# A one-token decode block: out projection in rows, PV of four groups in one PSUM tile, a fused mask-and-max, and a bf16 maximum broadcast

## The chip, the cores and the metric

The kernel runs on one core of a Trainium2 chip. The metric is device time in microseconds (us), median of the runs.

The profile is one execution recorded on the chip. Its span (first to last instruction) is some 2 us shorter than the device time. PE is the matmul engine, PEld its weight loads, DVE, ACT and POOL the vector, scalar and general engines, SP the engine that issues the loads.

## The reference, cut to what matters

```python
x = A_x                                       # [2, 1, 640], two sequences, one new token each
# layernorm, then attention over the last W = 2048 of 8192 cached tokens
q = (ln(x) @ wq).reshape(2, 1, 32, 192)       # wq 640 x 6144
scores = einsum("bhqd,bhkd->bhqk", q, k_cache[:, :, -2048:]) * 192 ** -0.5
o = einsum("bhqk,bhkd->bhqd", softmax(scores), v_cache[:, :, -2048:])
h = x + o.reshape(2, 1, 6144) @ wo            # wo 6144 x 640
# layernorm, then a gated feed-forward block of width 1536
out = h + (gelu(ln(h) @ w_gate) * (ln(h) @ w_up)) @ w_down
```

All of it is bf16. There are 64 pairs of sequence and head, 16 groups of 4. A group's K and V are 3.1 MB each, so K and V are 100 of the 122 MB that have to be read. There is one query row per head, so almost all the work is reading.

## The kernel before: the parts that matter here

Loads go through a ring of 120 KB per partition (five K or V tiles). SP issues the next load when the space that it needs has been used. The order is K0, wq, K1, V0, K2, V1, and so on, two of the four wo blocks in between, and at the end the other two, w_gate, w_up and w_down, the last in four pieces.

```python
WDC = ((0, 4), (4, 8), (8, 10), (10, 12))     # pieces of w_down
...
load_k(0); load_wq(); load_k(1)
for g in range(NG):
    if g > 0 and g + 1 < NG:
        load_k(g + 1)
    load_v(g)
    if g % 4 == 3 and g < NG - 5:
        load_wo(g // 4)
load_wo(2); load_wo(3); load_ffn()
```

For each group PE transposes K (48 matmuls of 128x128, two bf16 in an fp32), makes scores, and multiplies the exponentials with V:

```python
def scores(g):                                 # before
    def fn(e):
        for ch in range(4):                    # 4 matmuls that add -1e9 to the unwanted columns
            e.matmul(sps[32 * ch:32 * ch + 16, :], lhsT=mskl[:, :], rhs=mskr..., start=True, ...)
        for k in range(6):
            for ch in range(4):
                ins = e.matmul(sps[32 * ch:32 * ch + 16, :], lhsT=rq[:, g, k, :], rhs=ktr..., ...)
    ...
    dve(lambda e: e.tensor_reduce(out=mx[:, :], in_=sps[:, :], axis=AX.X, op=ALU.max), ...)

def pv(g):                                     # 32 matmuls of 384 columns into ops_, one eviction a group
    ...
    act(lambda e: e.activation(out=osb[:, :], in_=ops_[:, 0:384], func=ACT.Copy), ...)

def o_rows(g):                                 # fp32, once a group, accumulated over four groups
    ...

def oproj(J):                                  # wo is stationary, 2 columns move: 60 matmuls a block
    for kk in range(12):
        for c in range(NC5):
            ins = e.matmul(m2[:, 32 + 2 * c:34 + 2 * c], lhsT=wo[:, kk, c:D:NC5], rhs=ot[:, J % 2, kk, :], ...)
```

The end of the kernel is `oproj(2)`, `oproj(3)`, the second layernorm (`hnT`), the gate and up projections of 60 matmuls each, the product `uT`, and w_down: 48 matmuls, the last 8 of which need the last piece.

## Time and profile before

| | before |
|---|---|
| device time, median of 3 | 297.40 us (297.35 to 297.43) |
| span, mean granted clock | 295.3 us, 0.834 |
| PE, PEld, DVE, ACT busy | 74%, 60%, 42%, 36% |
| loads | 122.29 MB, 97.1% of 16 DMA engines' span |

These are lines of the page of the kernel before: busy time of the engines, DMA busy share in 40 slices (in tenths) with the rate, the DMA queues (packets, MB, share of 16 engines' span), and the chain of work that ended last, by engine and by line.

```profile
span 295.3 us, 5662 instructions
...
PE 219.8 (74%) x2537; PEld 175.8 (60%) x2537; DVE 125.2 (42%) x295; ACT 105.1 (36%) x138; POOL 1.0 (0%) x17
...
DMA  7999999999999999999999999999999999999992
GB/s 273 434 443 428 436 429 425 425 423 432 433 423 439 429 432 422 429 425 426 426 429 425 443 429 435 428 423 425 433 426 432 432 426 432 423 429 426 418 389 78
...
q1 hardware_dynamic: 6488, 122.29, 97.1%
q8 instruction: 20, 0.33, 0.4%
q14 instruction: 3, 0.02, 0.0%
...
DMA 68%; PE 25%; DVE 2%; ACT 2%; SPq 1%; issue 0%
DMA ring<-in_A_k_cache_dram 49%; PE tps L466 18%; DMA ring<-in_B_w_down_dram 10%; DMA ring<-in_A_wq_dram 9%; PE ops L566 2%; PE m L609 2%; PE sps L529 1%; ACT ktr L475 1%; ACT qrow L496 1%; DVE rq L319 1%; SPq L264 1%; PE m L597 1%; DVE mx 
```

What to read. DMA is at nine tenths or more from the second slice to the last but one. Between 41 and 250 us the windows view gives 429 GB/s at a DMA share of 1.01 (single slices of the page show up to 443 GB/s; how the view gives bytes to slices is not known). So the loads leave the DMA engines no pause in these 209 us, and the chain ends in w_down. That the engines could not move more than this was not shown. Two small queues, q8 and q14, are of the kind "instruction": they are taken to be the engines' code, 20 packets of 16384 bytes on q8 and 3 of 8192 bytes on q14. They move 0.35 MB in all.

These are the groups that the change touches, from the groups of instructions. A line gives busy us, mean ns of one, and idle time of the engine just before them with what ended it.

```profile
L466 PE MATMUL tps<-identf,ring 128*128 128x128 f32 x768 | 114.0, 317 | 41.5 <-DMA ring<-in_A_k_cache_dram 40.8
...
L580 PE MATMUL m<-osb,selw 128*128 128x192 f32 x64 | 14.7, 352 | 0.6 <-ACT osb L573 0.6
...
L535 DVE TENSOR_REDUCE mx<-sps 128x1 f32<-128x512 f32 x16 | 11.1, 692 | 46.2 <-PE sps L529 46.2
...
L609 PE MATMUL m<-ot,ring 128*128 128x2 bf16 x240 | 10.1, 178 | 1.0 <-DMA ring<-in_A_wo_dram 1.0
...
L573 ACT ACTIVATE osb<-ops 128x384 f32<-128x384 f32 x16 | 7.9, 491 | 20.7 <-PE ops L566 20.7
L524 PE MATMUL sps<-mskr,mskl 128*16 128x512 bf16 x64 | 7.0, 425 | 3.8 <-DVE mskl L315 3.8
...
L539 PE MATMUL m<-mrhs,pm 128*128 128x16 f32 x32 | 6.5, 280 | 2.6 <-DVE mrhs L315 1.1
```

The first line is the steady state: PE waited 41 us for K before the transposes.

This is the end in the timeline (start us, duration us, engine, line, operation, count, and in brackets the wait before it).

```profile
269.37 2.73 PE L566 MATMUL ops<-ring,ering 128*8 128x384 bf16 x32 [1.81 <-DMA ring<-in_A_v_cache_dram]
...
278.41 2.53 PE L609 MATMUL m<-ot,ring 128*128 128x2 bf16 x60 [0.99 <-DMA ring<-in_A_wo_dram]
...
283.80 0.17 DVE L319 TENSOR_TENSOR hnT<-dT,lt 128x10 bf16<-128x10 f32 x1 [1.21 <-ACT lt L368]
...
287.56 2.16 PE L664 MATMUL ops<-hnT,ring 128*128 128x2 bf16 x60 [1.00 <-DMA ring<-in_B_w_up_dram]
...
289.99 1.84 PE L695 MATMUL m<-ring,uT 128*2 128x160 bf16 x40 [0.27 <-DVE uT L319]
...
292.18 0.44 PE L695 MATMUL m<-ring,uT 128*2 128x160 bf16 x8 [0.34 <-DMA ring<-in_B_w_down_dram]
...
293.02 0.66 SPq L703 DMA_DIRECT2D out_dram<-yrow  x1
```

The last V is multiplied at 269.4 us. The up projection waits for its weights until 287.6 us, and the last 8 matmuls wait for the last piece of w_down until 292.2 us. From there to the end are about 3 us: an eviction, the store and its landing.

One thing is not in any view, but in the trace's records of semaphores: each of the 45 loads of the ring has 16 landing times on its semaphore, read here as one from each of 16 DMA engines. For K0 they lie within 0.6 us. For the last piece of w_down the first is at 287.31 us and the last at 292.13 us: some engines are 4.8 us behind others. Eight are at most 2.0 us behind the first, five are 3.4 us behind, three 4.6 us or more. The work waits for the last of them: the last 8 matmuls start at 292.18 us, 0.05 us after the landing at 292.13.

### The profile page before, as it was taken

To read this page: it belongs to the slowest core of one execution; us is meant where nothing else is said; L and a number is where in the kernel's file an instruction comes from. 1 tells how busy PE (TensorE), PEld (TensorE's weight loads), DVE (VectorE), ACT (ScalarE), POOL (GpSimd) and SP (SyncE) were. 2 spreads that over 40 slices of the span, in tenths; PEclk is the share of its full clock that TensorE was granted. 3 is DMA by queue.
4 is the path that set the end of the run, shared out by engine and by line. 5 is a ranking of instruction groups with operands and counts; after the bars stand their busy time and mean duration, and the time that the engine had idled before them with its cause. 6 is when DMAs were issued, how large, how long until landed. Compare 5 with 4: busy or idle time off the path is not lost.

```text
span 295.3 us, 5662 instructions
## 1 busy us (share of the span) xinstructions
PE 219.8 (74%) x2537; PEld 175.8 (60%) x2537; DVE 125.2 (42%) x295; ACT 105.1 (36%) x138; POOL 1.0 (0%) x17
## 2 busy tenths in 40 slices
PE   2573369989696399988493699987696978795865
PEld 1561239759393396865382695775676776672853
DVE  5640276545255151634264152563256434253230
ACT  2150306545353061735161241743344444341000
POOL 1000000000000000000000000000000000000000
PEclk9998757997979587999988597999597979597655
DMA  7999999999999999999999999999999999999992
GB/s 273 434 443 428 436 429 425 425 423 432 433 423 439 429 432 422 429 425 426 426 429 425 443 429 435 428 423 425 433 426 432 432 426 432 423 429 426 418 389 78
DMA packets 6523, 122.65 MB, mean 415 GB/s; under 512 B 738, under 2 KB 740, under 8 KB 1252
## 3 DMA queue, kind: packets, MB, share of 16 engines
q1 hardware_dynamic: 6488, 122.29, 97.1%
q8 instruction: 20, 0.33, 0.4%
q14 instruction: 3, 0.02, 0.0%
q10 hardware_dynamic: 12, 0.00, 0.0%
HBM read 122.29 MB, written 0.00 MB: 414 GB/s over the span
## 4 chain that ended last, share of the span: by engine, by line
DMA 68%; PE 25%; DVE 2%; ACT 2%; SPq 1%; issue 0%
DMA ring<-in_A_k_cache_dram 49%; PE tps L466 18%; DMA ring<-in_B_w_down_dram 10%; DMA ring<-in_A_wq_dram 9%; PE ops L566 2%; PE m L609 2%; PE sps L529 1%; ACT ktr L475 1%; ACT qrow L496 1%; DVE rq L319 1%; SPq L264 1%; PE m L597 1%; DVE mx L535 0%; PE sps L524 0%; PE m L539 0%
## 5 line engine op out<-in xcount | busy, mean ns | idle before, releaser
L466 PE MATMUL tps<-identf,ring 128*128 128x128 f32 x768 | 114.0, 317 | 41.5 <-DMA ring<-in_A_k_cache_dram 40.8
L466 PEld LDWEIGHTS tps<-identf,ring 128*128 128x128 f32 x768 | 105.8, 166 | 44.4 <-DMA ring<-in_A_k_cache_dram 42.0
L475 ACT ACTIVATE ktr<-tps 128x1024 bf16<-128x1024 bf16 x80 | 79.4, 1023 | 81.3 <-PE tps L466 80.6
L478 DVE COPY ktr<-tps 128x1024 bf16<-128x1024 bf16 x112 | 74.3, 688 | 65.6 <-PE tps L466 64.8
L566 PE MATMUL ops<-ring,ering 128*8 128x384 bf16 x512 | 27.4, 362 | 4.6 <-DMA ring<-in_A_v_cache_dram 4.4
L535 DVE TENSOR_REDUCE mx<-sps 128x1 f32<-128x512 f32 x16 | 11.1, 692 | 46.2 <-PE sps L529 46.2
L543 ACT ACTIVATE eexp<-sps,nm 128x512 bf16<-128x512 f32 x16 | 11.0, 687 | 51.5 <-DVE nm L541 48.7
L529 PE MATMUL sps<-ktr,rq 128*16 128x512 bf16 x384 | 26.2, 408 | 0.0
L566 PEld LDWEIGHTS ops<-ring,ering 128*8 128x8 bf16 x512 | 11.8, 92 | 15.6 <-issue 4.4
L529 PEld LDWEIGHTS sps<-ktr,rq 128*16 128x16 bf16 x384 | 10.1, 93 | 11.8 <-issue 2.8
L573 ACT ACTIVATE osb<-ops 128x384 f32<-128x384 f32 x16 | 7.9, 491 | 20.7 <-PE ops L566 20.7
L580 PE MATMUL m<-osb,selw 128*128 128x192 f32 x64 | 14.7, 352 | 0.6 <-ACT osb L573 0.6
L580 PEld LDWEIGHTS m<-osb,selw 128*128 128x128 f32 x64 | 10.0, 189 | 8.1 <-issue 6.8
L609 PE MATMUL m<-ot,ring 128*128 128x2 bf16 x240 | 10.1, 178 | 1.0 <-DMA ring<-in_A_wo_dram 1.0
L609 PEld LDWEIGHTS m<-ot,ring 128*128 128x128 bf16 x240 | 10.0, 131 | 1.1 <-DVE ot L601 1.0
L488 PE MATMUL tps<-ring,xnT 128*32 128x384 bf16 x80 | 5.0, 403 | 7.1 <-DMA ring<-in_A_wq_dram 5.9
L524 PE MATMUL sps<-mskr,mskl 128*16 128x512 bf16 x64 | 7.0, 425 | 3.8 <-DVE mskl L315 3.8
L319 DVE TENSOR_TENSOR rq<-ops,mask 128x96 bf16<-128x96 f32 x16 | 2.7, 246 | 15.2 <-PE ops L509 15.2
L539 PE MATMUL m<-mrhs,pm 128*128 128x16 f32 x32 | 6.5, 280 | 2.6 <-DVE mrhs L315 1.1
L488 PEld LDWEIGHTS tps<-ring,xnT 128*32 128x32 bf16 x80 | 2.4, 112 | 9.6 <-DMA ring<-in_A_wq_dram 7.0
L319 DVE TENSOR_TENSOR orow<-m,wm 128x1536 bf16<-128x1536 f32 (+2 forms) x5 | 8.0, 1597 | 0.2
L539 PEld LDWEIGHTS m<-mrhs,pm 128*128 128x128 f32 x32 | 5.0, 195 | 4.8 <-DVE mrhs L315 4.8
(97 smaller groups left out, 91.1 us busy)
## 6 DMA issues: line engine op xcount, KB each, us to landing
ring<-in_A_k_cache_dram SPq DMA_DIRECT2D x16, 3072.0 KB, 27.8
ring<-in_A_v_cache_dram SPq DMA_DIRECT2D x16, 3072.0 KB, 28.7
ring<-in_A_wo_dram SPq DMA_DIRECT2D x4, 1920.0 KB, 31.0
ring<-in_A_wq_dram SPq DMA_DIRECT2D x2, 3072.0 KB, 21.0
ring<-in_B_w_gate_dram SPq DMA_DIRECT2D x1, 1920.0 KB, 35.2
ring<-in_B_w_up_dram SPq DMA_DIRECT2D x1, 1920.0 KB, 25.9
ring<-in_A_wq_dram SPq DMA_DIRECT2D x1, 1536.0 KB, 27.9
ring<-in_B_w_down_dram SPq DMA_DIRECT2D x2, 640.0 KB, 27.5
```

The costliest lines, as they stand in the source:

```text
L319: return lambda e: e.tensor_tensor(out=out, in0=a, in1=b, op=op)
L466: ins = e.transpose(tps[bi][:, 128 * u:128 * (u + 1)], kv[:, off:off + 128], identf[:, :])
L475: act(lambda e, dst=dst, bv=bv: e.activation(out=dst, in_=bv, func=ACT.Copy), W=[("kt", slot, n)], X=[("t", bi)])
L478: dve(lambda e, dst=dst, bv=bv: e.tensor_copy(dst, bv), W=[("kt", slot, n)], X=[("t", bi)])
L529: ins = e.matmul(sps[32 * ch:32 * ch + 16, :], lhsT=rq[:, g, k, :], rhs=ktr[:, g % 2, k // 2, 1024 * ch + k % 2:1024 * (ch + 1):2], start= ...
L535: dve(lambda e: e.tensor_reduce(out=mx[:, :], in_=sps[:, :], axis=AX.X, op=ALU.max), W=["mx"], X=["s"])
L539: pe(lambda e: e.matmul(m2[:, 256:272], lhsT=pm[:, :], rhs=mrhs[:, :], start=True, stop=True), R=["pm", "mrhs"], X=["m2"])
L543: act(lambda e: e.activation(out=eexp[:, :], in_=sps[:, :], func=ACT.Exp, bias=nm[:, 0:1], scale=1.0, accum_out=zr[:, g % 2, :]), R=["nm"] ...
L566: ins = e.matmul(ops_[32 * r:32 * r + 8, 0:384], lhsT=ering[:, g % 2, t, :], rhs=vv[:, 384 * t:384 * (t + 1)], start=(t < 4), stop=(t >= 2 ...
L573: act(lambda e: e.activation(out=osb[:, :], in_=ops_[:, 0:384], func=ACT.Copy), W=["osb"], X=["o"])
L580: e.matmul(m1[:, 0:DH], lhsT=selw[:, tp, w:w + 128], rhs=osb[:, DH * tp:DH * (tp + 1)], start=(g % 4 == 0 and tp == 0), stop=(g % 4 == 3 a ...
L609: ins = e.matmul(m2[:, 32 + 2 * c:34 + 2 * c], lhsT=wo[:, kk, c:D:NC5], rhs=ot[:, J % 2, kk, :], start=(kk == 0 and c == 0), stop=(kk == 1 ...
```

## The change

The intent is to take work from PE, ACT and DVE:

- the mask becomes an addend of a fused DVE op (add, then maximum), which writes the masked scores to SBUF, and 64 mask matmuls go;
- the broadcast of the maximum goes from fp32 (32 matmul records for the 16 groups, so two passes each) to bf16;
- PV of four groups accumulates in one PSUM tile, each group in its own 8 of 32 stationary columns, so that eviction and `o_rows` come once for four groups;
- in the out projection the 2 columns of the attention output are stationary and wo moves, 24 matmuls of 320 columns a block instead of 60 of 2 columns. The result is in rows, is summed in SBUF with the residual, and `h_columns` turns it into columns for the layernorm.

```diff
-            pe(fn, R=[("rq", g), "mskl", "mskr"] + [("kt", g % 2, n) for n in range(12)], X=["s"])
-            dve(lambda e: e.tensor_reduce(out=mx[:, :], in_=sps[:, :], axis=AX.X, op=ALU.max), W=["mx"], X=["s"])
+            pe(fn, R=[("rq", g)] + [("kt", g % 2, n) for n in range(12)], X=["s"])
+            dve(lambda e: e.tensor_tensor_reduce(
+                out=sm[:, :].rearrange("p (u x) -> p u x", u=4), in0=sps[:, :].rearrange("p (u x) -> p u x", u=4),
+                in1=mska[:, :].unsqueeze(1).to_broadcast([128, 4, 128]), scale=1.0, scalar=-2.0 * BIG, op0=ALU.add, op1=ALU.max,
+                accum_out=mx[:, :]), R=["mska"], W=["sm", "mx"], X=["s"])
 ... (pm and mrhs become BF16)
-                    ins = e.matmul(ops_[32 * r:32 * r + 8, 0:384], lhsT=ering[:, g % 2, t, :],
-                                   rhs=vv[:, 384 * t:384 * (t + 1)], start=(t < 4), stop=(t >= 28),
+                    ins = e.matmul(ops_[32 * r:32 * (r + 1), 0:384], lhsT=ering[:, g % 4, t, :],
+                                   rhs=vv[:, 384 * t:384 * (t + 1)], start=(g % 4 == 0 and t < 4),
+                                   stop=(g % 4 == 3 and t >= 28),
 ... (eviction and o_rows only where g % 4 == 3)
                 for kk in range(12):
-                    for c in range(NC5):
-                        ins = e.matmul(m2[:, 32 + 2 * c:34 + 2 * c], lhsT=wo[:, kk, c:D:NC5], rhs=ot[:, J % 2, kk, :],
-                                       start=(kk == 0 and c == 0), stop=(kk == 11), skip_group_check=True)
+                    for h in range(2):
+                        r = 2 * (kk % 2) + h
+                        ins = e.matmul(m1[32 * r:32 * r + 2, 192:512], lhsT=ot[:, J % 2, kk, :],
+                                       rhs=wo[:, kk, 320 * h:320 * (h + 1)], start=..., stop=...,
+                                       tile_position=(0, 32 * r), skip_group_check=True)
+            if J % 2:
+                dve(tt(hrow[0:98, :], m1[0:98, 192:512], hrow[0:98, :], ALU.add), ...)
+        def h_columns():
+            ... (10 fp32 matmuls: lhsT=hrow[0:98, c:320:NC5], rhs=hsel[0:98, h, :])
 ... (constants, and the residual's rows for the end, in the same way)
```

The loads and their order are not touched.

## The prediction

> **What bounds the kernel now.** The DMA engines. The page's slices show DMA at nine tenths or more from the second slice to the last but one, its queue table gives queue 1 97.1% of 16 engines' span, and 122.3 MB pass at 414 GB/s over the span (some 430 GB/s in the windows of 5 us). [...] The landings come every 7.3 us for each 3 MB load, without a gap. The chain of waits is 68% DMA and ends in the last w_down landing at 292.1 us, the last 8 matmuls, one eviction and the store (about 3 us). PE is 74% busy, DVE 42%, ACT 36%.

> **What the change removes, adds, moves.** By the groups of instructions: 64 mask matmuls (7.0 us of PE), three quarters of the selw rows (14.7) and zsel rows (4.5), 12 of 16 osb evictions (5.9 of 7.9 us on ACT), half of the 32 fp32 max matmuls (6.5). The max reduction (692 ns x16) becomes a fused add-and-max with an SBUF output; I expect 0.7 to 1.0 us each, at most 5 us more on DVE. The out projection goes from 240 matmuls of 2 columns to 98 of 320 or so; from PV (32 of 384 columns in 1.5 us at full clock, 2.7 at half) I estimate 1.0 to 1.7 us per block against 2.5. PV itself, now 32 stationary columns, should not change. A POOL clear of 8 KB per partition falls into the start.

> Nearly all of this is hidden: no byte less is loaded, and in the steady part PE already waits 41 us for K. I expect PE busy around 195 us and more idle time before the transposes, and no earlier landings.

> **What can move the end.**
> (1) Instruction fetch. The trace's DMA records show 20 fetches of 16 KB, one per about 256 PE instructions (5100 in all[...]), and each puts one of the 16 engines about 1.4 us behind. They rotate over 8 engines, so by the end the last landing of a load trails its first by 4.8 us: three fetches on one engine. The change removes, by my count, 286 matmuls with their loads, 572 instructions, so 18 fetches remain. The 17th falls inside the up projection, near 287 us, still ahead of that engine's w_down bytes. So most of the gain is missed; V of group 15, wo and gate should land some 1.4 us earlier, the last w_down 0 to 1.4 us earlier.
> (2) The compute tail. After V 15: eviction, rows, a full-width orow (1.76 us instead of 0.96), columns, two projections without a wait between, then the new add over 320 columns, fp32 h_columns (20 passes, 1 to 2 us) and the copy. Estimate: normalised h at 282.5 to 285 us, against 284.0; up projection still about when its weights land. Hence the tail is nearly as long as the DMA.

> **Prediction: 297.0 us** (296.0 to 298.1 eight times in ten). Within 2%: 0.97; faster 0.01; slower 0.02.

> **Right or wrong would show as:** DMA share still 97%, the same 7.3 us cadence; the chain still ending in w_down; PE busy down 20 to 30 us with no change of span; 18 instruction fetches.

> **What would make it wrong:** the fused DVE op taking several times the 692 ns, so that a group's work exceeds its 14.6 us of loads; a ring slot released late enough to empty the queue; a tail longer by over 2 us (h_columns or the full-width orow at half clock); or the last engine losing its third fetch and the tail keeping up, which gives about 1.4 us.

## The result, and the profile after

| | before | after |
|---|---|---|
| device time, median | 297.38 us (297.26 to 297.43, 6 runs) | 297.29 us (297.10 to 297.44, 6 runs) |
| ratio | | 0.9997, 95% interval 0.9984 to 1.0010 |
| PE, PEld, DVE, ACT busy | 219.8, 175.8, 125.2, 105.1 us | 199.6, 158.1, 126.9, 99.8 us |
| PE code blocks fetched (q8) | 20 | 17 |
| last w_down landing | 292.13 us | 292.13 us |

Nothing was gained or lost. These are the lines of the page after that answer to those before.

```profile
span 295.3 us, 5104 instructions
...
PE 199.6 (68%) x2251; PEld 158.1 (54%) x2251; DVE 126.9 (43%) x313; ACT 99.8 (34%) x126; POOL 2.7 (1%) x18
...
DMA  7999999999999999999999999999999999999991
...
q1 hardware_dynamic: 6488, 122.29, 97.1%
q8 instruction: 17, 0.28, 0.4%
...
DMA 74%; PE 19%; DVE 3%; ACT 2%; SPq 1%; issue 0%
```

PE lost 20 us of work, 17.7 us of weight loads and 572 instructions (matmuls and loads), ACT lost 5 us, and the share of DMA is the same 97.1%. Code went from 20 blocks to 17. These are groups of the kernel after.

```profile
L464 PE MATMUL tps<-identf,ring 128*128 128x128 f32 x768 | 118.6, 325 | 48.1 <-DMA ring<-in_A_k_cache_dram 47.6
...
L529 DVE CUSTOM_DVE_ANT_1 sm<-sps,mska 128x512 f32<-128x512 f32 x16 | 11.1, 691 | 38.7 <-PE sps L523 38.7
...
L611 PE MATMUL m<-ring,ot 128*2 128x320 bf16 x96 | 5.5, 382 | 0.0
...
L536 PE MATMUL m<-mrhs,pm 128*128 128x16 bf16 x16 | 2.9, 184 | 16.9 <-DVE mrhs L319 16.1
...
L627 PE MATMUL m<-hsel,hrow 98*64 98x2 f32 x20 | 1.3, 255 | 0.6 <-DVE hrow L323 0.6
```

The saved work became waiting, as the steady state is paced by the loads. The smaller part of it is the wait for K before the transposes, 47.6 us instead of 40.8. The larger part is the wait for DVE's maximum before its broadcast, 16.1 us instead of 1.1: `o_rows`, which had filled this wait in every group, now comes once in four, and PE waits 13 times, once for each group without it. The transposes themselves take 325 ns on average where they took 317, so 4.6 us of what was saved went back. The fused DVE op takes 691 ns, the same as the plain maximum, plus 82 ns to read out its accumulator. A block of the out projection takes 1.0 us in the middle of the kernel (granted clock 1.00 there) and 1.8 us at the end (3.53 for two, clock 0.50), instead of 2.5.

And this is the end, in the timeline of the kernel after.

```profile
267.77 1.62 PE L565 MATMUL ops<-ring,ering 128*32 128x384 bf16 x32 [0.89 <-DMA ring<-in_A_v_cache_dram]
...
275.20 3.53 PE L611 MATMUL m<-ring,ot 128*2 128x320 bf16 x48
...
279.32 1.30 PE L627 MATMUL m<-hsel,hrow 98*64 98x2 f32 x20 [0.59 <-DVE hrow L323]
...
283.07 0.17 DVE L323 TENSOR_TENSOR hnT<-dT,lt 128x10 bf16<-128x10 f32 x1 [1.01 <-ACT lt L373]
...
286.04 2.16 PE L675 MATMUL ops<-hnT,ring 128*128 128x2 bf16 x60
...
288.55 0.70 PE L705 MATMUL m<-ring,uT 128*2 128x160 bf16 x16 [0.34 <-DVE uT L323]
...
290.59 1.23 PE L705 MATMUL m<-ring,uT 128*2 128x160 bf16 x24 [1.33 <-DMA ring<-in_B_w_down_dram]
...
292.17 0.44 PE L705 MATMUL m<-ring,uT 128*2 128x160 bf16 x8 [0.35 <-DMA ring<-in_B_w_down_dram]
...
293.01 0.65 SPq L713 DMA_DIRECT2D out_dram<-yrow  x1
```

The last V is multiplied 1.6 us earlier than before, and the up projection starts 1.5 us earlier. But the product with w_down, which started at 290.0 us and now starts at 288.6 us, comes to a halt after 16 matmuls, and the last 8 start at 292.17 us, where they started at 292.18 us. Everything in the tail moved forward except the last landing. So the question is what sets that one time.

### The profile page after: what moved, and what is told of

The parts are those of the page before. It is cut to its first block, busy times and chain, and to the rows that moved or that the text cites. A ratio compares the mean times of both kernels' runs of the same rounds, so it can differ in the third digit from the quotient of the medians.

```text
span 295.3 us, 5104 instructions
## 1 busy us (share of the span) xinstructions
PE 199.6 (68%) x2251; PEld 158.1 (54%) x2251; DVE 126.9 (43%) x313; ACT 99.8 (34%) x126; POOL 2.7 (1%) x18
## 3 DMA queue, kind: packets, MB, share of 16 engines
q1 hardware_dynamic: 6488, 122.29, 97.1%
## 4 chain that ended last, share of the span: by engine, by line
DMA 74%; PE 19%; DVE 3%; ACT 2%; SPq 1%; issue 0%
DMA ring<-in_A_k_cache_dram 54%; PE tps L464 17%; DMA ring<-in_B_w_down_dram 10%; DMA ring<-in_A_wq_dram 9%; SPq L268 1%; ACT qrow L494 1%; PE ops L565 1%; DVE rq L323 1%; ACT ktr L473 1%; PE m L611 0%; PE m L594 0%; PE m L549 0%; PE tps L486 0%; DVE ktr L476 0%; DVE cf L323 0%
## 5 line engine op out<-in xcount | busy, mean ns | idle before, releaser
L464 PE MATMUL tps<-identf,ring 128*128 128x128 f32 x768 | 118.6, 325 | 48.1 <-DMA ring<-in_A_k_cache_dram 47.6
L464 PEld LDWEIGHTS tps<-identf,ring 128*128 128x128 f32 x768 | 109.4, 171 | 51.4 <-DMA ring<-in_A_k_cache_dram 48.9
L540 ACT ACTIVATE eexp<-sm,nm 128x512 bf16<-128x512 f32 x16 | 11.5, 722 | 63.4 <-DVE nm L538 63.4
L529 DVE CUSTOM_DVE_ANT_1 sm<-sps,mska 128x512 f32<-128x512 f32 x16 | 11.1, 691 | 38.7 <-PE sps L523 38.7
L565 PE MATMUL ops<-ring,ering 128*32 128x384 bf16 x512 | 23.9, 328 | 3.6 <-DMA ring<-in_A_v_cache_dram 3.5
L565 PEld LDWEIGHTS ops<-ring,ering 128*32 128x32 bf16 x512 | 12.5, 96 | 11.8 <-DMA ring<-in_A_v_cache_dram 4.6
L536 PE MATMUL m<-mrhs,pm 128*128 128x16 bf16 x16 | 2.9, 184 | 16.9 <-DVE mrhs L319 16.1
L323 DVE TENSOR_TENSOR ering<-m,mask 128x256 bf16<-128x256 f32 x16 | 6.7, 420 | 3.2 <-PE m L549 3.2
L323 DVE TENSOR_TENSOR orow<-m,wm 128x1536 bf16<-128x1536 f32 x4 | 7.0, 1757 | 0.1
L594 PE MATMUL m<-selb,orow 128*128 128x2 bf16 x48 | 3.5, 200 | 4.1 <-DVE orow L323 2.5
L549 PE MATMUL m<-sel,eexp 128*128 128x64 bf16 x64 | 5.0, 206 | 1.2 <-ACT eexp L540 1.2
```

The lines of the kernel that those rows point to most:

```text
L323: return lambda e: e.tensor_tensor(out=out, in0=a, in1=b, op=op)
L464: ins = e.transpose(tps[bi][:, 128 * u:128 * (u + 1)], kv[:, off:off + 128], identf[:, :])
L529: dve(lambda e: e.tensor_tensor_reduce(out=sm[:, :].rearrange("p (u x) -> p u x", u=4), in0=sps[:, :].rearrange("p (u x) -> p u x", u=4), ...
L540: act(lambda e: e.activation(out=eexp[:, :], in_=sm[:, :], func=ACT.Exp, bias=nm[:, 0:1], scale=1.0, accum_out=zr[:, g // 4 % 2, g % 4:g % ...
L549: ins = e.matmul(o, lhsT=eexp[:, 128 * u:128 * (u + 1)], rhs=sel64[:, :], start=True, stop=True)
L565: ins = e.matmul(ops_[32 * r:32 * (r + 1), 0:384], lhsT=ering[:, g % 4, t, :], rhs=vv[:, 384 * t:384 * (t + 1)], start=(g % 4 == 0 and t < 4),
```

## The experiments

**Rival A**: bytes alone set the end, and code is too little to matter. **Rival B**: PE work counts somewhere, and a gain was given back somewhere else. **Rival C**: the new tail (orow over the full width, `h_columns`) ends the kernel.

### One block of code less

```diff
-                for k in range(6):
+                for k in range(4):                     # scores of 4 of 6 slices: wrong on purpose
-                                       stop=(k == 5), tile_position=(0, 32 * ch))
+                                       stop=(k == 3), tile_position=(0, 32 * ch))
```

> The changed kernel with the scores of 4 of 6 k slices (a wrong result on purpose): 256 PE instructions less, so that 16 instead of 17 blocks of code are fetched, and no engine fetches three. Theory (the end is set by the DMA engine that has fetched most PE code): last w_down landing about 290.7 us instead of 292.1, time 1.2 to 1.5 us less, about 295.9 us. Rival A (the bytes of the loads alone set the end; code fetches are hidden): 297.3 us, landing at 292.1. Rival B (PE work itself is what is hidden or not): 7 us of PE are gone as they were in the change, nothing gained, 297.3 us.

Measured: 295.88 us (295.75 to 296.41, 4 runs), before 297.38, ratio 0.9950 (0.9935 to 0.9965). These are the code queue of its page, and the last matmuls of its timeline.

```profile
q8 instruction: 16, 0.26, 0.4%
```

```profile
288.87 1.50 PE L705 MATMUL m<-ring,uT 128*2 128x160 bf16 x40 [0.34 <-DVE uT L323]
...
290.68 0.43 PE L705 MATMUL m<-ring,uT 128*2 128x160 bf16 x8 [0.30 <-DMA ring<-in_B_w_down_dram]
```

Sixteen fetches, and the last piece of w_down is there 1.5 us earlier. No load was changed. Rival A falls. (The comparison with the reference passed here too: the scores of these inputs are so small that it can't tell a wrong score from a right one.)

The same cut in the kernel before:

> The kernel before with the same cut that gave 1.5 us on the changed kernel (scores of 4 of 6 k slices, 256 PE instructions less, a wrong result on purpose): 4870 PE instructions, so 18 code fetches before the up projection's end instead of 19, and two engines still have three. Theory: last w_down landing still about 292.1 us, time 297.4 us, within 0.3. Rival (the cut work itself gave the 1.5 us): 295.9 us.

Measured: 297.40 us (297.35 to 297.50, 4 runs), before 297.39, ratio 1.0000 (0.9983 to 1.0017). The same work taken away gave 1.5 us on one kernel and nothing on the other. That is rival B answered: it isn't the work.

### More code, no more work

Narrow weight loads that nothing uses, on PE where it waits:

```diff
+        def early(e):                                  # at the start, and again before q_stationary
+            for _ in range(212):
+                ins = e.ldweights(identb[:, 0:2])
+            return ins
 ...
         def softmax(g):
-            pe(lambda e: e.matmul(m2[:, 256:272], lhsT=pm[:, :], rhs=mrhs[:, :], start=True, stop=True), ...)
+            def fn(e):
+                ins = e.matmul(m2[:, 256:272], lhsT=pm[:, :], rhs=mrhs[:, :], start=True, stop=True)
+                for _ in range(40 if g > 0 else 0):
+                    e.ldweights(selb[:, :])
+                return ins
```

> The changed kernel with 1024 extra narrow weight loads on PE where it is idle: 21 fetches instead of 17, so five of the eight engines have three instead of one, and none four. Theory: the last landing depends on the worst engine alone, so it stays at 292.1 to 292.4 us and the time at 297.3 us within 0.4. A rival in which every fetch costs the DMA as a whole its share would give 4 times 1.1 us over 16 engines, 0.3 us more.

Measured: 297.42 us (297.25 to 297.66, 4 runs), ratio 0.9999 (0.9984 to 1.0014). 21 fetches, five engines with three, and the same end.

With 424 and 80 in place of 212 and 40:

> The changed kernel with 2048 extra narrow weight loads: 25 fetches, the first of the eight engines has four. Theory: last landing about 293.5 us, time 1.2 to 1.5 us more, about 298.7 us. Rival A: 297.3 us. A rival in which only the mean over 16 engines counts: 8 times 1.1 us over 16, 0.55 us more, 297.9 us.

Measured: 299.84 us, but from 298.75 to 301.22 in 4 runs, ratio 1.0082 (1.0050 to 1.0115). This is a miss of the design. In the windows view (busy us of each engine, granted clock, DMA share, GB/s) the loads slow down early on:

```profile
core 0: us, PE busy (x) PEld busy (x) DVE busy (x) ACT busy (x) POOL busy (x), PEclk, DMA share, GB/s
...
50.00:67.00 17.00, 14.96 (x146) 13.78 (x227) 9.22 (x18) 9.09 (x12) 0.00 (x0) 0.85 0.93 381
67.00:80.00 13.00, 10.96 (x131) 9.49 (x213) 7.84 (x16) 7.14 (x9) 0.00 (x0) 1.00 0.99 425
```

The loads at the start held up PE, ring space came free late, and the DMA queue ran dry for a while. The first landing of the last piece moved from 287.5 to 289.8 us, and the 25th fetch came only at 292.7 us, after everything. The trailing of the last landing was 4.87 us, as with three fetches. The run says nothing about a fourth. But it shows that the empty queue wiped the lag out here: in the load that landed at 60.0 us the last engine was 2.23 us behind the first, and in the next one, at 69.4 us, all but one were within 0.47 us. It was made again, with 208 at the start only and 130 a group:

> The changed kernel with 2158 extra narrow weight loads, 130 in each group's wait for K and only 208 at the start, so that the loads of K and V are not held up as they were in the first trial (its queue ran dry between 52 and 66 us). The 25th code fetch falls some 310 instructions before the end and gives one engine its fourth. Theory: last landing trails its first by about 6.2 us instead of 4.6, time about 298.7 us. Rival (mean over the engines): 297.9 us. Rival A: 297.3 us.

Measured: 298.90 us (298.44 to 298.99, 4 runs), before 297.39, ratio 1.0048 (1.0033 to 1.0063). These are its code queue and its last matmuls:

```profile
q8 instruction: 26, 0.43, 0.6%
```

```profile
293.44 0.43 PE L717 MATMUL m<-ring,uT 128*2 128x160 bf16 x8 [0.35 <-DMA ring<-in_B_w_down_dram]
```

The 25th fetch was at 287.6 us, and the last matmuls start 1.3 us later than in the kernel after. The 26th was at 291.9 us, when it mattered to nobody. The loads were not held up this time: the first landing of the last piece was at 287.39 us, and at 287.52 us in the kernel after.

All of these runs but the first trial with 2048 loads can be put in one table. "In time" are the fetches that started before 290.5 us, "trailing" is the last less the first of the 16 landings of the last piece of w_down, and the last column counts the engines that trail by over 4 us.

| run | fetches in time | last landing, us | trailing, us | engines over 4 us behind | device time, us |
|---|---|---|---|---|---|
| changed kernel, one block less | 16 | 290.63 | 3.35 | 0 | 295.88 |
| changed kernel | 17 | 292.13 | 4.61 | 1 | 297.29 |
| kernel before, one block less | 18 | 292.35 | 4.96 | 2 | 297.40 |
| changed kernel, PE time put back (below) | 18 | 292.21 | 4.97 | 2 | 297.33 |
| kernel before | 19 | 292.13 | 4.82 | 3 | 297.38 |
| changed kernel, 1024 loads more | 21 | 292.20 | 4.88 | 5 | 297.42 |
| changed kernel, 2158 loads more | 25 | 293.40 | 6.01 | 8 | 298.90 |

The number of engines over 4 us behind is the number of fetches less 16, up to 8, in every row, and in the last row one engine is 6.01 us behind. The run left out has 24 fetches in time and only three such engines; 19 of the 24 came from 63.9 us on, when its queue had run dry, and 19 less 16 is three. The time goes in steps: one engine with a third fetch is as bad as five. The first third fetch moved the last landing by 1.5 us and the device time by 1.4 us, the first fourth by 1.3 and 1.6 us. How a DMA engine divides its time between code and loads was not shown. Which of the 16 engines these are is not in the trace's records. That they are eight is read from the landings and the durations. Why a fetch of 1.0 to 1.1 us puts the last landing back by 1.3 to 1.5 us stays open.

### PE time put back

```diff
         def scores(g):
             def fn(e):
+                for _ in range(8):
+                    e.matmul(sps[:, :], lhsT=identb[:, :], rhs=ktr[:, g % 2, 0, 0:512], start=True, stop=True)
```

> The changed kernel with 8 extra matmuls of 512 columns a group ahead of the scores, their result overwritten: about 27 us of PE time put back, more than the change took away, and 256 instructions, so 18 fetches and still three at most on one engine. Theory: 297.3 us, within 0.4. If PE time in the middle counted, up to 20 us more.

Measured: 297.33 us (297.29 to 297.35, 4 runs), ratio 0.9998 (0.9983 to 1.0013). These are PE's busy time and the code queue on its page:

```profile
PE 216.3 (73%) x2379; PEld 151.8 (51%) x2379; DVE 126.3 (43%) x313; ACT 99.1 (34%) x126; POOL 2.7 (1%) x18
...
q8 instruction: 18, 0.29, 0.4%
```

PE is busy 16.7 us longer than in the kernel after, and the time is the same. The added matmuls alone are 32.1 us on the page (27 us had been estimated). But the granted clock was higher, 0.90 instead of 0.83, and the transposes took 295 ns instead of 325. So more work than the change took from PE can be put back at no cost.

### Does the tail end the kernel?

A pad on DVE between the up projection and its product with the gate:

```diff
+        for k in range(2):                             # 4 in the third run
+            dve(lambda e: e.tensor_copy(padt[:, :, :], ops_[:, 0:24].unsqueeze(2).to_broadcast([128, 24, 21])), W=["pad"], X=["o"])
         dve(tt(uT[:, :, :]..., ops_[:, 0:2 * NF], ga[:, 0, :], ALU.mult), ...)
```

> The changed kernel with two copies of 128x504 on DVE, some 1.2 to 1.5 us, between the up projection and its product with the gate. The third w_down load ends the idle time of PE at 290.6 us, and 40 matmuls from 288.6 take 1.5 us, so the tail has about 2.1 us of slack. Theory (the DMA ends the kernel): 297.3 us, nothing lost. Rival (the new tail ends it): 1.2 to 1.5 us more.

> The kernel before with the same two copies. Its w_down matmuls start at 290.0 us, so its slack is about 0.7 us. Theory: 0.6 to 1.0 us more, about 298.2 us: the change bought slack in the tail that the time does not show.

> The changed kernel with four copies, some 2.5 to 3 us. Theory: 0.4 to 0.9 us more than 297.3 us, as the slack of about 2.1 us is used up. Rival (the tail ends it): 2.5 to 3 us more.

| pad | on | device time, us | before in the same rounds | ratio |
|---|---|---|---|---|
| 2 copies, 1.40 us | after | 298.03 (297.97 to 298.36, 4 runs) | 297.39 | 1.0022 (1.0007 to 1.0037) |
| 2 copies, 1.40 us | before | 297.92 (297.72 to 297.97, 4 runs) | 297.39 | 1.0015 (0.9998 to 1.0031) |
| 4 copies, 2.83 us | after | 298.30 (297.92 to 298.69, 4 runs) | 297.39 | 1.0029 (1.0014 to 1.0044) |

The pad of 2.83 us cost 1.0 us on the changed kernel, where the theory had 0.4 to 0.9 and rival C 2.5 to 3. The pad of 1.40 us cost 0.5 us on the kernel before, a little less than the 0.6 to 1.0 that were expected (the interval just includes no change, but all four runs lie above the seven without the pad). But on the changed kernel it cost 0.7 us, where nothing was expected, so the theory was wrong for this run. Its timeline shows that the tail kept up all the same:

```profile
288.26 1.40 DVE L700 CAST padt<-ops 128x504 bf16<-128x504 f32 x2 [0.91 <-PE ops L677]
...
292.21 0.44 PE L709 MATMUL m<-ring,uT 128*2 128x160 bf16 x8 [0.35 <-DMA ring<-in_B_w_down_dram]
...
293.05 0.65 SPq L717 DMA_DIRECT2D out_dram<-yrow  x1
```

The last 8 matmuls start at 292.21 us and the store is issued at 293.05 us, against 292.17 and 293.01 us without the pad. And yet the span is 296.3 us and not 295.3: SP's wait for the store ended at 295.84 us instead of 294.87 us. In each half of the store (SP issues one, ACT the other) the last landing came 0.9 us after the one before it; in the kernel after it was 0.03 us. In the DMA records there is a code block of 8192 bytes on q14 at 294.20 us, for 0.53 us. In the kernel after, this block comes at 296.39 us, when all is over. In the run with four copies it came at 284.6 us. The pad had added one instruction to DVE's program (328 instead of 327, as built), and so had moved the place where a new block is needed. That was a new theory and got two runs: the same pad with no instruction more, and an instruction more with next to no pad.

```diff
+        dve(lambda e: e.tensor_copy(orow...[:, 0:1008]..., ops_[:, 0:24].unsqueeze(2).to_broadcast([128, 24, 42])), W=["orow"], X=["o"])
```

> The two copies of the pad, which cost 0.7 us on the changed kernel although its last w_down matmul did not move (292.2 us), as one copy of 1008 columns, about 1.4 us as well, so that DVE has one instruction less (327 in place of 328). New theory: the 0.7 us came from a block of DVE code that was fetched at 294.2 us, while the output was stored; with one instruction less it falls after the end (296.4 us in the changed kernel). Expects 297.3 us, within 0.2. Rival (the pad's time itself counts): 298.0 us.

```diff
+        for k in range(2):
+            dve(lambda e: e.tensor_copy(padt[:, :], ops_[:, 0:1]), W=["pad"], X=["o"])    # padt is 128x1
```

> The changed kernel with two copies of one column at the place of the pad, some 0.1 to 0.2 us in all, and 328 DVE instructions. New theory: the DVE code block is fetched near 294.2 us again, the store lands about 1 us later, 297.9 to 298.2 us. Rival (the pad's time itself counts): 297.3 us.

Measured: one copy of 1.21 us, 297.31 us (297.10 to 297.66, 5 runs), ratio 0.9998 (0.9984 to 1.0011), the block at 296.45 us. Two copies of one column: 298.03 us (297.87 to 298.24, 5 runs), ratio 1.0022 (1.0010 to 1.0035), the block at 294.13 us. The end of the latter in its timeline:

```profile
288.76 0.36 DVE L700 CAST padt<-ops 128x1 bf16<-128x1 f32 x2 [0.88 <-PE ops L677]
...
292.16 0.44 PE L709 MATMUL m<-ring,uT 128*2 128x160 bf16 x8 [0.34 <-DMA ring<-in_B_w_down_dram]
...
293.00 0.65 SPq L717 DMA_DIRECT2D out_dram<-yrow  x1
```

So a real pad of 1.2 us is free on the changed kernel, and two copies of one column cost 0.7 us. Rival C falls: the changed kernel's tail has over a microsecond to spare. What the first pad cost was a code block fetched while the output was stored. That the block is DVE's is inferred, from the instruction that moved it and from the blocks at 15.65 and 138.89 us in the kernel after, between which DVE began 126 instructions (8192 bytes are 128, if 16384 are 256). Why the fetch comes just then stays open.

### Can the load be balanced?

If eight engines are behind, they should get fewer of the last bytes. So the last two pieces of w_down were issued as 16 loads of 8 partitions each, in the expectation that 8 engines would carry each of them. The trace of this run has eight landings for each of these loads, where a whole piece has 16, and does not show which engines they are.

```diff
-                P.op("sp", lambda e, v=v, src=src: e.dma_start(v, src), ...)
+                parts = 16 if key in (("wd", 2), ("wd", 3)) else 1
+                def fn(e, ...):
+                    w = 128 // parts
+                    for j in range(parts):
+                        ins = e.dma_start(v[w * j:w * (j + 1)], src[w * j:w * (j + 1)]) if parts > 1 else e.dma_start(v, src)
+                        ...
```

> The changed kernel with the last two w_down loads (327 KB each) in 16 pieces of 8 partitions, so that each piece is spread over 8 engines and not 16. Theory: if these 8 engines are not the 8 that fetch PE code, the load is balanced and the last landing comes about 1.5 us earlier (time about 295.8 us); if they are the same 8, it comes about 1.5 us later (298.8 us); if half are, no change or somewhat later. Rival A (no engine lags because of code): 8 engines carry the double for 0.65 MB, so about 1.5 us later in any case.

Measured: 302.25 us (302.24 to 303.15, 4 runs), ratio 1.0171 (1.0154 to 1.0188). None of the expectations. The landings show why it says nothing about the balance: the parts of the last piece landed between 289.7 and 296.9 us, one after another, where the whole piece in one load lands between 287.5 and 292.1 us. Loads as small as 20 KB (2560 bytes on each of 8 engines) had a cost of their own here that hides any gain: in the DMA records a packet of 2560 bytes took 0.10 us in the kernel after, and here 0.17 us in the median and 0.20 us at the end. Whether the engines used are those that fetch code stays open.

### A version that beats both?

The cut kernel shows what there is to gain: 1.4 us, if PE's program stays under its 17th block until w_down is in, that is, by an estimate from where the boundaries lie, some 200 to 260 PE instructions less than the changed kernel has. A correct way wasn't found. What could be saved by counting (bf16 for `h_columns` and the last rows, w_down in 320 columns) is some 100 instructions, and gate and up projections in rows would lengthen the tail by more, by an estimate from the durations above, than there is to gain. No such version was run.

## Why the prediction was right

The prediction said 297.0 us, from 296.0 to 298.1, and 0.97 for "within 2%". Measured were 297.29 us. Point by point:

- *"Nearly all of this is hidden: no byte less is loaded."* Right. The DMA share stayed at 97.1%, PE's wait for K grew from 40.8 to 47.6 us and its wait for DVE's maximum from 1.1 to 16.1 us (the prediction had named only the first), and 16.7 us of PE busy time put back cost nothing.
- *"18 fetches remain. The 17th falls inside the up projection, near 287 us, still ahead of that engine's w_down bytes."* The mechanism was right, the count was not: 17 remained. The step that failed is the subtraction: 572 instructions are 2.2 blocks, and 20 less 2.2 was taken as 18. But the 20th boundary had only just been crossed (5100 instructions are 19.9 blocks, and 20.0 to 20.2 with the 20 to 80 instructions by which the boundaries lie earlier), so three boundaries went and not two. The 17th came at 288.2 us, as the up projection ended, and made one engine the last. The number survived the wrong count by luck: the fetch that mattered was the 17th, and it was there with either count.
- *"V of group 15, wo and gate should land some 1.4 us earlier, the last w_down 0 to 1.4 us earlier."* The last V was multiplied 1.6 us earlier, the up projection started 1.5 us earlier, the last w_down landed 0.0 us earlier. The point of 297.0 us held some hope for that range. It is a step and not a range: with one third fetch all is lost, without it all is won (295.88 us).
- *"PE busy around 195 us."* 199.6 us. The transposes, taken as unchanged, cost 4.6 us more (325 ns instead of 317), which is about the difference. But the multiplications with V, also taken as unchanged, cost 3.5 us less (328 ns instead of 362), so the sum is not accounted for in full.
- *"0.7 to 1.0 us each"* for the fused op: 0.69 us and 0.08 us for its accumulator. *"1.0 to 1.7 us per block"* of the projection: 1.0 us in the middle and 1.8 us at the end, so just outside. *"20 passes, 1 to 2 us"* for `h_columns`: 1.3 us. *"Normalised h at 282.5 to 285 us"*: the op that makes it started at 283.1 us.
- *"Hence the tail is nearly as long as the DMA."* Too cautious. A pad of 1.2 us in the tail is free. The estimate let the up projection start about when its weights landed, which was right, but the weights landed 1.5 us earlier and the last w_down didn't, and that gap is the slack.

Where did 20 us of PE work go, then? Into waiting in the steady part: 15.0 us more for DVE's maximum and 6.8 us more for K. At the end, some 1.5 us of the tail were won by fewer code fetches before it and then lost to the one fetch that remained.

## What to carry to other kernels

In this kernel the loads filled 97.1% of the DMA engines' span, and work taken from the engines in the middle (20.2 us of PE's busy time) was worth nothing in itself (297.29 us for 297.38). What is left in such a case is the first bytes, the last bytes, and whatever else the same DMA engines carry. Look at the 16 landing times of the last load, not at the mean DMA share: here one engine was 4.6 us behind the first, and the mean said 97%. Instructions were DMA traffic too: here one block of code, fetched at 288.2 us, 4 us before the last landing, held up one engine and moved the whole end by 1.4 us. So count the instructions of each engine, and see where the last block boundary falls, before believing a change of a microsecond in the tail.
